# Pooled products with the last 16 keys: four of 32 rows and 72 columns in place of two of 64 padded rows and 144 columns

## The chip, the cores and the metric

The kernel runs on one core of a Trainium2 chip. The metric is the device time of one execution, in microseconds (us), as the median of several. The engines are TensorE (PE; its weight loads are shown apart as PEld), VectorE (DVE), ScalarE (ACT), GpSimd (POOL) and SyncE (SP, which here only issues DMAs).

## What is computed

Attention over 8 batches and 8 heads, 576 positions, 64 elements a head, followed by a layer of two matrix products with a gate. The attention is a sum of two parts: one on sequences pooled by four (144 pooled queries, keys and values), repeated four times, and one inside a band of seven positions.

```python
q_d = q.reshape(B, H, Sd, 4, D).mean(axis=3)      # k_d, v_d alike; Sd = 144
out_d = softmax(q_d @ k_d.T / 8) @ v_d
out_up = np.repeat(out_d, 4, axis=2)
mask = np.abs(pos[:, None] - pos[None, :]) < 4
out_local = softmax(np.where(mask, q @ k.T / 8, -1e9)) @ v
x = (out_up + out_local)                          # to (4608, 512)
h = x @ w_in                                      # 512 -> 2048
out = (h * np.clip(h + 3, 0, 6) / 6) @ w_out      # 2048 -> 512
```

## The kernel before

The attention is done in units: one unit is one batch and a pair of heads, so there are four units in each of the eight batches. The first batch (b = 0) and the second (b = 1) take other paths; from the third batch on (b = 2 to 7, the units for which `alone` is false) 24 units go through the path that the change touches. The two heads of a pair are called h = 0 and 1; their 64 elements lie on the lower and the upper 64 partitions.

A planner (`Plan`) puts all pieces of work in order. Every piece has a cost in us, what it depends on, which buffers it takes and frees, and a due time; the planner simulates five queues with them and then writes out each engine's instructions in that order. The costs are numbers in the calls of `op(...)`.

The expert layers (lines 1065 and 1124) are products of 128 rows and 128 columns on 512 moving columns. Each weight and each activation is split in a high and a low part, so that each product is made of three. Between these, TensorE does the units in bursts (`plan_burst`): one burst does the scores of a new unit and the products with v of a unit that came two before. In the order of the code a burst is:

- `scores_d4` (line 507): the pooled scores of the new unit;
- `pv` (line 747): 20 banded products of the old unit. The window of 57 to 64 keys on one half of the partitions is the row half g of the array, the head h the column half, so that four products in turn use the four quarters;
- `pv_d4` (line 671): the pooled products of the old unit, described below;
- `scores` (line 704): 20 banded scores of the new unit.

The last two bursts have only an old unit, that is `pv` and `pv_d4`.

Between its scores and its products a unit's pooled probabilities are written to DRAM by rows of queries (`put_d`) and fetched back in blocks of 32 by 32 (`get_d`, lines 618 to 631), and DVE turns each block over (`turn_d`, line 633), so that keys lie on partitions. The tile `rd` has 18 blocks of 32 columns. The first 12 hold keys 0 to 127 of both heads, on 128 partitions. Blocks 12 to 17 hold the last 16 keys (`KR`), 16 of head 0 and 16 of head 1 on 32 partitions, with 64 queries in each of three parts, of which 48 (`QB`) are used. The three parts overlap (they begin 40 queries apart, `QSTEP`), and `used` picks the 48.

The pooled values are sums of four rows of v (`ld4` and `sum4`). Part g = 0 has pooled keys 0 to 127. For part g = 1, the last 16 keys, `ld4` (lines 436 to 438) loads the same 16 rows twice, onto partitions 0 to 15 and 16 to 31; `sum4` sums them, multiplies each head's 64 columns by a column of `head` (line 455), which is one on that head's 16 partitions and zero on the other's, and clears rows 32 to 63 (line 456).

`pv_d4` (lines 661 to 673) then does three steps, each for both heads: g = 0 takes keys 0 to 63, g = 1 keys 64 to 127, both with 64 rows and 144 queries, into the two PSUM banks `pod[0]` and `pod[1]`; g = 2 takes the last keys on partitions 0 to 63, rows 32 to 63 being zero, with 144 queries, and adds into `pod[0]`. Heads use the two column halves. The banks are added afterwards by `mean` and `mean_too` (lines 684 to 689).

In the second batch (`mixed`) `pv_d4` does g = 2 with 48 rows instead; the change leaves that as it is.

Of the kernel before, what the change touches and what calls it, by code (L numbers as in the profile page):

```python
# [8 lines left out]
F32 = mybir.dt.float32  # L9
# [5 lines left out]
ALU = mybir.AluOpType  # L15
AX = mybir.AxisListType

B, H, S, D = 8, 8, 576, 64
DM, DFF = 512, 2048
P = 128  # L20
# [7 lines left out]
SD = S // 4  # L28
# [3 lines left out]
ROW = 2 * D  # L32
# [3 lines left out]
NAR = 32  # L36
QS, QSTEP, QB = 64, 40, 48
# [2 lines left out]
QPLACE = ((0, 0), (0, 2), (1, 1)), ((0, 1), (1, 0), (1, 2))  # L40
KR = SD - P
KEEP = NAR + KR
MASKED = -8.0e9
FIRST4 = 4 * STEP // 4
FOURS = FIRST4 + 1 + SD // 2
# [14 lines left out]
def tile_local_down_attention_moe(ctx, tc, q_all, k_all, v_all, _qk_loc, _v_loc, w_in, w_out, ident_d, _mask_d, out):  # L60
# [7 lines left out]
    nc = tc.nc  # L68
# [4 lines left out]
    const = pool("const")  # L73
# [9 lines left out]
    ident = const.tile([P, P], F32, name="ident")  # L83
# [3 lines left out]
    op = plan.op  # L87
# [7 lines left out]
    def buf(key, holder, shape):  # L95

        n = 1
        for k in shape[1:]:
            n *= k
        slot = plan.slot[key, holder]  # L100
        if type(slot[0]) is str:
            tag, first = PLACES[slot[0]]
            if tag not in early:
                early[tag] = wts.tile([P, 2048 if PAIRED[0] <= int(tag[1:]) < PAIRED[1] else 1024], F32, name="early", tag=tag)
            return view(early[tag][:, first + slot[1] // 4:], n, shape)
        at = slot[0]
        if at < XB:
            place = key if key == "rawd" else "xb"
            if place not in early:
                early[place] = mem.tile([P, XB // 4], F32, name="first", tag="first")  # L110
            return view(early[place][:, at // 4:], n, shape)
        t, at = (arena, at - XB) if at < ARENA else (rounded, at - ARENA)
        return view(t[:, at // 4:], n, shape)
# [13 lines left out]

    hot = const.tile([P, P], BF16, name="hot")
    mask = const.tile([P, D], F32, name="mask")
    head = const.tile([NAR, 2], F32, name="head")  # L130

    def scratch():
        if "zz" not in early:
# [30 lines left out]

    def make_head():
        for h in range(2):
            nc.vector.tensor_reduce(out=head[:, h:h + 1], in_=ident[:NAR, h * KR:(h + 1) * KR], op=ALU.add, axis=AX.X)


    win, wout = {}, {}  # L170
# [71 lines left out]
    def src(t, first, ap):  # L242
        return bass.AP(tensor=t.tensor, offset=t.offset + first * ROW, ap=ap)
# [124 lines left out]
    def plan_unit(b, d, u, row0, k0, kv, PS, pair, masked, early_user, due):  # L368
        hp = 2 * d + u
        row0 = row0 + u * S  # L370
        un = b, hp
        st, qk = {}, {}
        s_ops, sd_ops, turned, pooled = [], [], {}, {}

        alone = un < ALONE

        direct = b == 0
        mixed = alone and not direct
# [29 lines left out]
        for kind, t in (("q", q_all), ("k", k_all)):  # L408
            hk = kind, un
            if direct:  # L410
                a = turned[kind] = pair["turned"][kind]
            else:
                l = op("SP", 2.0, partial(ldt, t, kind), loads if b == 1 else [], take=[("qk", hk)], size=dma(4 * S, 128), nd=4, each=0.57)
                a = turned[kind] = [op("DVE", 0.72, partial(turn, kind), [l])]
# [14 lines left out]
        def ld4(g):  # L429
            st["raw", g] = raw = buf("raw" + k0, ("v", un, g), [P, 4, ROW])  # L430
            if g == 0:
                nc.sync.dma_start(raw, src(v_all, row0, [[4 * ROW, P], [1, 4 * ROW]]))
            elif alone:
                nc.sync.dma_start(raw[NAR:KEEP], src(v_all, row0 + 4 * P, [[4 * ROW, KR], [1, 4 * ROW]]))
            else:
                for h in range(2):
                    nc.sync.dma_start(
                        raw[h * KR:(h + 1) * KR], src(v_all, row0 + 4 * P, [[4 * ROW, KR], [1, 4 * ROW]]))

        def sum4(g, eng):  # L440
            if "vd" not in st:
                st["vd"] = buf("vd" + k0, un, [P, 2, ROW])
            ps = slice(NAR, KEEP) if g and alone else slice(0, 2 * KR if g else P)
            raw, vd = raw_of(g)[ps], st["vd"][ps, g]
            if g and alone:
                eng.memset(st["vd"][:NAR, 1], 0.0)
            if eng is nc.vector:
                eng.tensor_reduce(out=vd, in_=raw.rearrange("p r e -> p e r"), op=ALU.add, axis=AX.X)  # L448
            else:
                eng.tensor_tensor(raw[:, 0:2], raw[:, 0:2], raw[:, 2:4], op=ALU.add)  # L450
                eng.tensor_tensor(vd, raw[:, 0], raw[:, 1], op=ALU.add)
            if g and not alone:

                for h in range(2):
                    eng.tensor_scalar(vd[:, h * D:(h + 1) * D], vd[:, h * D:(h + 1) * D], head[:, h:h + 1], None, op0=ALU.mult)
                eng.memset(st["vd"][NAR:D, 1], 0.0)

        def v_of():
            return pair["v"][:, u] if b == 0 else st["v"]
# [156 lines left out]
                    st["pd"][h * D:(h + 1) * D])  # L616

        def get_d():
            st["rd"] = raw = buf("qk", ("rd", un), [P, 18, NAR])
            st["pdt"] = raw.rearrange("p j k -> p (j k)")  # L620
            dd = st["dd"]
            for e in range(4):
                nc.sync.dma_start(
                    raw[e * NAR:(e + 1) * NAR, :12],
                    bass.AP(tensor=dd.tensor, offset=dd.offset + e * NAR, ap=[[SD, NAR], [NAR * SD, 12], [1, NAR]]))
            for h in range(2):
                for i in range(2):
                    nc.sync.dma_start(
                        raw[:NAR, 12 + i::2, h * KR:(h + 1) * KR],
                        bass.AP(tensor=dd.tensor, offset=dd.offset + (h * D + i * NAR) * SD + P,  # L630
                                ap=[[SD, NAR], [2 * D * SD, 3], [1, KR]]))

        def turn_d(i):
            n, a, e = (P, 0, 12 * NAR) if i == 0 else (NAR, 12 * NAR, 18 * NAR)
            x = st["pdt"][:n, a:e]
            nc.vector.transpose(out=x, in_=x)

# [19 lines left out]
        def used(x, first, step):  # L657

            return bass.AP(tensor=x.tensor, offset=x.offset + first, ap=[x.ap[0], [step + QB - QSTEP, 3], [1, QB]])

        def pv_d4():

            st["od"] = buf("od" + k0, un, [P, SD])
            st["pod"] = [st["px"][g][:, HALF:HALF + SD] for g in range(2)]
            for g in (0, 1, 2):
                ks = slice(0, KEEP) if mixed and g == 2 else slice(g % 2 * D, (g % 2 + 1) * D)
                for h in range(2):
                    hs = slice(h * D, (h + 1) * D)
                    w = used(st["pdt"][ks, g // 2], h * D, 2 * D) if mixed else \
                        used(st["pdt"][ks], h * D, 2 * D) if g < 2 else used(st["pdt"][ks], 6 * D, D)  # L670
                    nc.tensor.matmul(  # L671
                        st["pod"][g % 2][hs].rearrange("p (j q) -> p j q", j=3), st["vd"][ks, g // 2, hs],
                        w, start=(g < 2), stop=(g > 0), skip_group_check=True)

        def pv_d():
            st["pod"] = bank(PS, ("od", un))[:, :SD]
# [142 lines left out]
        elif alone:  # L819
            a = op("DVE", 0.52, lambda: top(rows_d(), st["md"]), [sd])  # L820
            sums_d = [op("ACT", 1.6, lambda: weigh(rows_d(), st["pd"], st["md"], st["sd"]), [a], free=[bk])]
        else:
            pulls = [op(on("ev", SD // 2), 0, partial(pull, h, i), [sd], take=[pk], free=[hx[h]]) for h in range(2) for i in range(2)]
            sums_d = []
            for n in (2, 0, 1):
                a = op("DVE", 0.22, lambda n=n: top(rows_d4(n), st["md"][:, n:n + 1]), pulls if n == 2 else [sd])
                sums_d.append(op("ACT", 0.84, partial(weigh4, n), [a], take=[pk], free=[bks[n]] if n != 2 else []))
        a = op("DVE", 0.15, lambda: recip(st["sd"]), sums_d)
        a = op(on("normd" if alone else "norm", 3 * SD), 0, lambda eng: norm(eng, st["pd"], st["sd"]), [a], free=[sk], lock=True)
# [1443 lines left out]
```

## Time and profile before

| | |
|---|---|
| time, median of 3 runs | 879.05 us (878.76 to 880.36) |
| profiled execution | span 877.4 us from the first to the last instruction; no other time is given for it |
| PE busy | 870.0 us (99%), 6964 products |
| PE weight loads | 716.1 us (82%) |
| DVE, ACT, POOL busy | 74%, 56%, 30% |
| chain that ended last | 98% PE |
| DMA | 136.40 MB, 155 GB/s over the span |

Times in the profile are from the start of the span. An f32 product shows as two records (each with its weight load), a product of the split kind as one. Records of products overlap, since products are pipelined: the distance between starts, or the pieces of the chain, tell how fast they follow each other, not the duration of a record. A form such as `64*64 64x144` is: 64 rows by 64 columns of the array, 64 partitions by 144 moving columns.

### The profile page before, as it was taken

To read this page: it belongs to the slowest core of one execution; us is meant where nothing else is said; L and a number is where in the kernel's file an instruction comes from. 1 tells how busy PE (TensorE), PEld (TensorE's weight loads), DVE (VectorE), ACT (ScalarE), POOL (GpSimd) and SP (SyncE) were. 2 spreads that over 40 slices of the span, in tenths; PEclk is the share of its full clock that TensorE was granted. 3 is DMA by queue.
4 is the path that set the end of the run, shared out by engine and by line. 5 is a ranking of instruction groups with operands and counts; after the bars stand their busy time and mean duration, and the time that the engine had idled before them with its cause. 6 is when DMAs were issued, how large, how long until landed. Compare 5 with 4: busy or idle time off the path is not lost.

```text
span 877.4 us, 19829 instructions
## 1 busy us (share of the span) xinstructions
PE 870.0 (99%) x6964; PEld 716.1 (82%) x6964; DVE 651.5 (74%) x1235; ACT 494.3 (56%) x1557; POOL 264.3 (30%) x396
## 2 busy tenths in 40 slices
PE   8999999999999999999999999999999999999998
PEld 5788888888888888888888888888888888888887
DVE  7997976766876787667766776667856768778984
ACT  5998856575564555545454555555552325556760
POOL 6646542423324331344323431433422110000000
PEclk9999999999999999999999999999999999999999
DMA  9899253675766665656465647677864116674794
GB/s 250 238 312 254 65 129 89 126 142 117 147 155 132 138 125 129 130 118 135 100 156 127 134 105 167 133 195 221 195 148 104 37 39 234 207 227 145 268 274 71
DMA packets 358735, 136.40 MB, mean 155 GB/s; under 512 B 269612, under 2 KB 331180, under 8 KB 358636
## 3 DMA queue, kind: packets, MB, share of 16 engines
q1 hardware_dynamic: 353052, 134.22, 61.7%
q10 hardware_dynamic: 5584, 0.92, 0.6%
q8 instruction: 55, 0.90, 0.4%
q14 instruction: 44, 0.36, 0.1%
HBM read 90.44 MB, written 44.63 MB: 154 GB/s over the span
## 4 chain that ended last, share of the span: by engine, by line
PE 98%; DMA 0%; DVE 0%; issue 0%; SPq 0%; ACT 0%
PE o L1124 36%; PE h L1065 35%; PE a L1381 4%; PE h L1381 4%; PE o L1644 4%; PE o L1491 2%; PE a L704 2%; PE h L747 2%; PE a L507 1%; PE h L1644 1%; PE a L1644 1%; PE h L671 1%; DMA arena<-in_q_dram 0%; PE a L597 0%; PE h L507 0%; PE a L747 0%
## 5 line engine op out<-in xcount | busy, mean ns | idle before, releaser
L1124 PE MATMUL o<-wp,rounded 128*128 128x512 f32 x1344 | 323.6, 392 | 0.0
L1065 PE MATMUL h<-rounded,wp 128*128 128x512 f32 x1344 | 315.9, 390 | 0.0
L1065 PEld LDWEIGHTS h<-rounded,wp 128*128 128x128 f32 x1344 | 251.5, 188 | 52.6 <-issue 0.4
L1124 PEld LDWEIGHTS o<-wp,rounded 128*128 128x128 f32 x1344 | 249.6, 188 | 53.7 <-issue 1.0
L1075 DVE SCALAR_TENSOR_TENSOR arena<-arena,h 128x512 f32<-128x512 f32 x112 | 75.8, 677 | 54.9 <-ACT arena L1071 54.0
L1071 ACT ACTIVATE arena<-h 128x512 f32<-128x512 f32 x112 | 66.6, 595 | 83.3 <-PE h L1065 76.0
L1079 ACT CAST rounded<-arena 128x512 fp32r<-128x512 f32 x112 | 68.9, 616 | 63.3 <-PE o L1124 39.5
L1083 DVE TENSOR_TENSOR rounded<-arena,rounded 128x512 fp32r<-128x512 f32 x78 | 57.3, 735 | 48.5 <-PE o L1124 41.7
L571 ACT ACTIVATE arena<-arena 128x64 f32<-128x64 f32 x240 | 80.1, 336 | 0.4
L1083 POOL TENSOR_TENSOR rounded<-arena,rounded 128x512 fp32r<-128x512 f32 x34 | 46.2, 1359 | 96.8 <-PE o L1124 48.7
L1187 POOL TENSOR_TENSOR arena<-arena 128x128 f32<-128x128 f32 x65 | 33.1, 510 | 67.5 <-DVE arena L1187 38.6
L391 DVE STREAM_TRANSPOSE arena<-arena 128x576 f32<-128x576 f32 x56 | 42.8, 767 | 4.4 <-DMA arena<-in_q_dram 2.7
L571 ACT ACTIVATION_READ_ACCUMULATOR arena<-arena 128x1 f32 x240 | 45.3, 189 | 0.0
L547 ACT ACTIVATE arena<-arena 128x1 f32<-128x1 f32 (+1 forms) x77 | 14.9, 194 | 52.8 <-DVE arena L560 52.6
L450 POOL TENSOR_TENSOR arena<-arena 32x256 f32<-32x256 f32 (+2 forms) x28 | 21.4, 763 | 74.7 <-DMA arena<-in_v_dram 74.5
L685 ACT ACTIVATE arena<-h 128x144 f32<-128x144 f32 x24 | 7.0, 291 | 64.7 <-PE h L671 64.7
L448 DVE TENSOR_REDUCE arena<-arena 128x128 f32<-128x512 f32 (+2 forms) x28 | 29.7, 1063 | 6.9 <-PE h L671 5.6
L581 DVE RECIPROCAL arena<-arena 128x10 f32<-128x10 f32 (+1 forms) x60 | 11.4, 190 | 29.0 <-ACT arena L557 16.5
L588 DVE TENSOR_TENSOR arena<-arena 128x640 f32<-128x640 f32 (+1 forms) x38 | 31.8, 836 | 1.1
L560 DVE TENSOR_REDUCE arena<-arena 128x10 f32<-128x640 f32 (+1 forms) x57 | 31.3, 553 | 0.2
L406 POOL TENSOR_TENSOR arena<-arena 128x144 f32<-128x144 f32 x52 | 29.9, 575 | 4.1
L1381 PE MATMUL h<-wp,wp 128*128 128x512 f32 x120 | 30.0, 389 | 0.0
(286 smaller groups left out, 1371.0 us busy)
## 6 DMA issues: line engine op xcount, KB each, us to landing
rawp<-in_w_in_dram SPq DMA_DIRECT2D x16, 512.0 KB
rawp<-in_w_out_dram SPq DMA_DIRECT2D x16, 512.0 KB
arena<-in_q_dram SPq DMA_DIRECT2D x112, 72.0 KB
arena<-in_k_dram SPq DMA_DIRECT2D x112, 72.0 KB
pl<-arena SPq DMA_DIRECT2D x24, 320.0 KB
arena<-pl SPq DMA_DIRECT2D x96, 80.0 KB
arena<-in_v_dram SPq DMA_DIRECT2D x28, 256.0 KB
wd<-wp SPq DMA_DIRECT2D x12, 512.0 KB
```

The costliest lines, as they stand in the source:

```text
L391: nc.vector.transpose(out=qk[kind], in_=qk[kind])
L571: nc.scalar.activation(x[:, j], x[:, j], AF.Exp, bias=m[:, j:j + 1], scale=0.125, accum_out=s[:, j:j + 1])
L588: eng.tensor_tensor(x, x, s.unsqueeze(2).broadcast_to(list(x.shape)), op=ALU.mult)
L1065: nc.tensor.matmul(st["ps"], win[f][:, wt, kk * P:(kk + 1) * P], xs[part][:, kk], start=(kk == 0 and i == 0), stop=(kk == NK - 1 and i == ...
L1071: nc.scalar.activation(st["t"], st["ps"], AF.Relu, bias=3.0)
L1075: nc.vector.scalar_tensor_tensor(out=t, in0=t, scalar=6.0, in1=st["ps"], op0=ALU.min, op1=ALU.mult)
L1079: nc.scalar.copy(st["gh"], st["t"])
L1083: eng.tensor_tensor(st["gl"], st["t"], st["gh"].bitcast(F32), op=ALU.subtract)
L1124: nc.tensor.matmul(otile[n, m], gt[:, ms], wout[f][:, wt], start=(f == 0 and i == 0), stop=(f == NF - 1 and i == 2),)
L1187: eng.tensor_tensor(u[:, z], u[:, x], u[:, y], op=o)
L1381: nc.tensor.matmul(ps, weight(i, j, wt, kk), xpart(MOVING[j], part)[:, kk], start=first and kk == 0 and x == 0, stop=kk == half - 1 and x ...
L1644: nc.tensor.matmul(places[acc, m][:, ts], w, z[:, part, ts], start=j == 5 and i == 0 and x == 0, stop=i == NG - 1 and x == 2, skip_group_c ...
```

## The change

The last 16 keys are laid out twice: the first half of the queries of each part (24, `QH`) with its keys on partitions 0 to 31, the second half on partitions 64 to 95. The values of the last 16 keys are loaded to both places. `pv_d4` then does g = 2 with 32 rows from partition 0 and 72 queries (the first 24 of each part) into `pod[0]`, and g = 3 with 32 rows from partition 64 and the other 72 queries into `pod[1]`, each for both heads. Rows 32 to 63 are read by no product any more and are not cleared. `turn_d` turns 96 partitions by 96 columns in place of 32 by 192, `rd` has 15 blocks, and `sum4` works on 96 partitions for g = 1. All costs and dependences given to the planner stay as they are.

```diff
+QH = QB // 2
...
-    head = const.tile([NAR, 2], F32, name="head")
+    head = const.tile([P, 2], F32, name="head")
...
-            nc.vector.tensor_reduce(out=head[:, h:h + 1], in_=ident[:NAR, h * KR:(h + 1) * KR], op=ALU.add, axis=AX.X)
+            nc.vector.tensor_reduce(
+                out=head[:, h:h + 1], in_=ident.rearrange("p (g k) -> p g k", g=2)[:, :, h * KR:(h + 1) * KR], op=ALU.add, axis=AX.XY)
...
-                for h in range(2):
+                for i in range(2):
                     nc.sync.dma_start(
-                        raw[h * KR:(h + 1) * KR], src(v_all, row0 + 4 * P, [[4 * ROW, KR], [1, 4 * ROW]]))
+                        raw[i * D:i * D + NAR], src(v_all, row0 + 4 * P, [[0, 2], [4 * ROW, KR], [1, 4 * ROW]]))
...
-            ps = slice(NAR, KEEP) if g and alone else slice(0, 2 * KR if g else P)
+            ps = slice(NAR, KEEP) if g and alone else slice(0, D + NAR if g else P)
...
-                    eng.tensor_scalar(vd[:, h * D:(h + 1) * D], vd[:, h * D:(h + 1) * D], head[:, h:h + 1], None, op0=ALU.mult)
-                eng.memset(st["vd"][NAR:D, 1], 0.0)
+                    eng.tensor_scalar(vd[:, h * D:(h + 1) * D], vd[:, h * D:(h + 1) * D], head[ps, h:h + 1], None, op0=ALU.mult)
...
-            st["rd"] = raw = buf("qk", ("rd", un), [P, 18, NAR])
+            st["rd"] = raw = buf("qk", ("rd", un), [P, 15, NAR])
...
-                        raw[:NAR, 12 + i::2, h * KR:(h + 1) * KR],
-                        bass.AP(tensor=dd.tensor, offset=dd.offset + (h * D + i * NAR) * SD + P,
-                                ap=[[SD, NAR], [2 * D * SD, 3], [1, KR]]))
+                        raw[i * D:i * D + QH, 12:, h * KR:(h + 1) * KR],
+                        bass.AP(tensor=dd.tensor, offset=dd.offset + (h * D + i * QH) * SD + P,
+                                ap=[[SD, QH], [(2 * D + QB - QSTEP) * SD, 3], [1, KR]]))
...
-            n, a, e = (P, 0, 12 * NAR) if i == 0 else (NAR, 12 * NAR, 18 * NAR)
+            n, a, e = (P, 0, 12 * NAR) if i == 0 else (D + NAR, 12 * NAR, 15 * NAR)
...
-            for g in (0, 1, 2):
-                ks = slice(0, KEEP) if mixed and g == 2 else slice(g % 2 * D, (g % 2 + 1) * D)
+            for g in (0, 1, 2) if mixed else range(4):
+                n = KEEP if g == 2 and mixed else D if g < 2 else NAR
+                ks = slice(g % 2 * D, g % 2 * D + n)
                 for h in range(2):
                     hs = slice(h * D, (h + 1) * D)
-                    w = used(st["pdt"][ks, g // 2], h * D, 2 * D) if mixed else \
-                        used(st["pdt"][ks], h * D, 2 * D) if g < 2 else used(st["pdt"][ks], 6 * D, D)
+                    to = st["pod"][g % 2][hs].rearrange("p (j q) -> p j q", j=3)
+                    if g < 2 or mixed:
+                        w = used(st["pdt"][ks, g // 2] if mixed else st["pdt"][ks], h * D, 2 * D)
+                    else:
+                        w = st["rd"][ks, 12:, :QH]
+                        to = to[:, :, g % 2 * QH:(g % 2 + 1) * QH]
                     nc.tensor.matmul(
-                        st["pod"][g % 2][hs].rearrange("p (j q) -> p j q", j=3), st["vd"][ks, g // 2, hs],
-                        w, start=(g < 2), stop=(g > 0), skip_group_check=True)
+                        to, st["vd"][ks, g // 2, hs], w, start=(g < 2), stop=(g == 1 if mixed else g > 1) or g == 2, skip_group_check=True)
```

## Rows read from the trace of the kernel before

**Rows 1.** The page: busy time with share and instructions, granted clock, DMA totals.

```profile
PE 870.0 (99%) x6964; PEld 716.1 (82%) x6964; DVE 651.5 (74%) x1235; ACT 494.3 (56%) x1557; POOL 264.3 (30%) x396
...
PEclk9999999999999999999999999999999999999999
...
DMA packets 358735, 136.40 MB, mean 155 GB/s; under 512 B 269612, under 2 KB 331180, under 8 KB 358636
```

**Rows 2.** Stretches, PE alone: length, busy time and count, clock, DMA.

```profile
160.00:691.00 531.00, 531.00 (x4578) 1.00 0.62 139
691.00:873.70 182.70, 182.70 (x828) 1.00 0.57 176
```

**Rows 3.** Chain of waits around a burst: start, us, line and count.

```profile
301.17 2.72 PE o L1124 x12
...
306.07 2.95 PE o L1124 x12
...
330.83 0.41 PE a L507 x8
331.24 0.13 PE h L507 x8
331.36 0.58 PE h L747 x40
331.94 0.36 PE h L671 x10
332.30 0.04 PE a L704
332.34 0.09 PE h L671 x2
332.43 0.58 PE a L704 x29
```

**Rows 4.** Chain of waits, the last burst, which has no scores.

```profile
689.69 0.74 PE h L747 x40
690.43 0.48 PE h L671 x12
```

**Rows 5.** Chain of waits, a burst with scores alone.

```profile
138.02 0.58 PE a L704 x40
```

**Rows 6.** Lines 704 and 671, 160 to 691 us: durations, starts, forms.

```profile
L704 PE MATMUL a<-arena x880: 216/218/268, 168.6 to 647.0; 64*64 64x64 f32 x176
...
L671 PE MATMUL h<-arena x288: 282/283/294, 168.3 to 690.6; 64*64 64x144 f32 x144
```

**Rows 7.** Chain of waits, pooled products of the first and second batch.

```profile
34.52 0.64 PE a L682 x8
...
61.59 0.48 PE a L671 x12
```

**Rows 8.** Order of time on PE: start, us from first start to last end.

```profile
28.40 0.29 PE L682 MATMUL o<-early 72*64 72x144 f32 x1
28.61 0.27 PE L747 MATMUL o<-early 64*64 64x60 f32 x2
...
61.66 0.41 PE L671 MATMUL a<-first,arena 48*64 48x144 f32 x4
```

**Rows 9.** Groups by line and form: busy us, mean ns, idle time before.

```profile
L636 DVE STREAM_TRANSPOSE arena<-arena 128x384 f32<-128x384 f32 x24 | 13.7, 570 | 0.0
...
L450 POOL TENSOR_TENSOR arena<-arena 32x256 f32<-32x256 f32 x20 | 15.1, 756 | 73.0 <-DMA arena<-in_v_dram 73.0
...
L636 DVE STREAM_TRANSPOSE arena<-arena 32x192 f32<-32x192 f32 x24 | 7.8, 326 | 0.4 <-DMA arena<-pd 0.4
...
L450 POOL TENSOR_TENSOR arena<-arena 128x256 f32<-128x256 f32 x5 | 4.1, 812 | 1.5 <-DMA arena<-in_v_dram 1.5
```

**Rows 10.** Who waited for line 437's loads: us in all, times.

```profile
  POOL arena L450: 73.0, 8
```

**Rows 11.** DMA issues: line, count, KB each.

```profile
arena<-in_v_dram SPq DMA_DIRECT2D x80, 32.0 KB
```

## The prediction

> **What bounds the kernel now.** I read the page first: TensorE (PE) is busy for 870.0 of 877.4 us, no other engine for more than 74%, and PEclk stands at 9 in every slice, so all of what follows is at full clock [rows 1]. Busy time of PE is modelled, so I next asked for stretches: from 160 to 691 us, where all 24 changed units fall, PE is busy for 531.00 of 531.00 us, and from there to 873.7 for 182.70 of 182.70 [rows 2]. Then the chain of waits: from the first changed burst on it names nothing but PE lines, back to back; the reader sees in it one burst between two pieces of the expert layers, and no wait for DVE, ACT, POOL or a DMA [rows 3]. The kernel is therefore bound by the length of PE's own instruction stream. A change to that stream counts in full and everything else has slack. What matters is how long PE needs for the pooled products of a burst.
>
> In the chain a piece runs from the end of the piece before it to its own end, which makes lengths comparable. A burst runs: pooled scores (L507), banded products (L747), pooled products (L671), banded scores (L704). Each f32 product shows as two records. Four products in four different quarters of the array run side by side: 40 records of L747 take 0.58 us, or ten rounds of 0.058 [rows 3].
>
> **Pooled products without any other effect.** Before: first 128 keys, four products in four quarters; then the last 16 keys, two products, both in the upper row half, 144 columns. Twelve records take 0.48 us where nothing interleaves [rows 4], which is four rounds of 0.12, two for the first four products and two for the last two. After: the last keys are four products of 72 columns, one in each quarter. The price of that form is shown by L507 h, four products of 64x72 in the four quarters: 8 records in 0.13 us, against 0.24 for 144 columns [rows 3]. So I count 0.24 - 0.12 = 0.12 us less per burst. Does L704, which slips four records into the idle lower half, give this back? With the interleaving L704 takes 0.04 + 0.58 = 0.62 [rows 3]; a burst without pooled products takes 0.58 for all 40 records [rows 5]. The early start buys nothing, so the saving stays at 0.12 in both places. 24 bursts hold L671 (288 records at 12 each), 22 of them with L704 behind (880 records at 40 each) [rows 6].
>
> **What the change adds on PE: another tile height.** All products around it use 64 rows by 64 columns. The new ones use 32 rows. Nothing in this trace uses 32-row products, so the cost of going there and back must be bounded.
>
> Upper side: each time the kernel changes the shape in which the array is cut, PE loses time with no semaphore behind it. (a) From 128x128 products to 64x64 ones: L747 takes 0.74 us where it starts a burst [rows 4] and 0.58 inside one [rows 3], so 0.16 us. (b) The same step into L507: 0.41 for two rounds worth 0.24 [rows 3], 0.17. (c) From 64x64 (L747) to 72*64 products, whose 72 rows need the taller cut at equal columns: L682 takes 0.64 us for 8 records, two side by side, so four rounds worth 0.48, again 0.16 [rows 7]. (d) Back from 72*64 to 64x64: starts 0.21 us apart (28.40 to 28.61), where a round takes 0.12, so 0.09 of emptying before any exposed weight load [rows 8]. (e) From 64x64 to 128x128: L1124 x12 takes 2.95 behind a burst and 2.72 elsewhere, 0.23 [rows 3], with weights twice as wide.
>
> Lower side: a smaller row count alone costs nothing. In the bursts of batch 2 the last-key products have 48 rows [rows 8], and the twelve records take 0.48 us as where all have 64 [rows 7]. If 32 rows are to the array what 48 are, the switch is 0; nothing there suggests a gain beyond the 0.12.
>
> I take 0.16 per switch, by (a) to (c): 48 rows still fit a 64-row cut and 72 don't fit it; that is where the rows show the loss, and (c) is the nearest row, a change of height alone at 64 columns. 32 rows, cut in strips of their own, are such a change. The range keeps 0 and 0.23.
>
> Trainium skill, "TensorEngine Tiling (Array Packing)", section "Key Properties": going from one tiling mode to another (not from tile to tile) empties the engine; its "Available Configurations" list 32x64 apart from 64x64. The trace agrees for every change of cut that it holds (0.09 to 0.23 us, rows 3, 4, 7, 8); none of them is 64 to 32. By it the sum is the one below.
>
> **Sum.** In each of the 22 bursts with L704 behind there are two added switches: 2 x 0.16 - 0.12 = +0.20 us. In the last two bursts the array goes to 128x128 behind the pooled products anyway, so one switch is added: 0.16 - 0.12 = +0.04. 22 x 0.20 + 2 x 0.04 = 4.5 us. Profiled span 877.4 + 4.5 = 881.9. The page gives the profiled execution as its span only; the median of the runs, 879.05, stands 1.65 above it (what lies around the span), which doesn't change. Forecast: 883.5 us, 0.5% slower.
>
> **The other edits, all beside PE.**
> - Turning the last keys (L636): 32x192 becomes 96x96 on DVE. 32x192 takes 326 ns and 128x384 570 [rows 9]: with 192 columns more, 244 ns or 1.27 a column, so 96 columns take about 204 ns, an estimate from these two rows; 0.12 us less, 24 times. DVE isn't on the chain [rows 3]: 0 on the time.
> - Sums of v (L448 to L456): 96 partitions instead of 32 at equal width, and one memset less. POOL takes 756 ns for 32x256 and 812 for 128x256 [rows 9], so up to 56 more in L450; by the same ratio, 1.07, the other POOL operations of the unit grow by less than that each, and DVE's by the two rows above not at all. Bounds per unit: 0 (the memset pays for it) and 0.2 us, for four operations at 56 ns. The cover is POOL's idle time, 70% of the span by the page; without it 24 x 0.2 = 4.8 us. Value: 0.
> - Loads of v (L437): two issues of 32 KB [rows 11] become two of 64 KB, 1.5 MB more over 24 units. At the mean 155 GB/s [rows 1] 64 KB more take 0.4 us longer to land. POOL stands in L450 for these loads for 73.0 us in all, in 8 waits [rows 10], and what is queued behind on POOL (L451, L455, some L1083) stands with it; L1083's result is what PE needs next. Without cover that is 24 x 0.4 = 9.9 us. But those 8 waits of about 9 us each leave no mark on PE [rows 2], so 0.4 more stays hidden: 0.
> - Fetching probabilities (L628): still four issues, with 72 short runs each for 96. The SP queue issues as many as before and moves fewer bytes: 0.
> - head (L167) is made once, at the start, and gets wider by a hundred elements: 0. The cost terms that set the order are untouched, so nothing is moved past another queue.
> - Two more products per burst are 4 matmul records more, 96 on 6964 [rows 1], each with its weight load. PE never stood for its instructions between 160 and 873 us [rows 2]: 0.
>
> **Rivals.**
> 1. *The switch is free* (32 rows behave in a 64-row cut as 48 do). For it: the 48 rows [rows 7, 8], and the gapless moves between quarters [rows 3]. Against it: every crossing of a tile height in the trace costs [rows 4, 7, 8]. Time: 24 x -0.12 = -2.9, 876.2 us, faster. It decides as soon as a switch costs under 0.06 us. Trainium skill, "TensorE: Matmul & The Clock Gate", section "Part 3: Packing small matmuls — row/col tiling": slices that start at partition multiples of 32 land in row groups of their own and run together, with no word of a price for coming from another size. That the quarters run together the trace agrees (0.058 us a round, rows 3); the price is what it leaves open, and by this rule alone the sum would be this rival's. Chance 0.14.
> 2. *Only the emptying is paid*, 0.09 (d), and the weights are loaded meanwhile: 2 x 0.09 - 0.12 = +0.06, and -0.03 in the last two: 22 x 0.06 - 0.06 = 1.3 us, 880.3. For it: the load of the next weights runs beside products elsewhere. Against it: (a) to (c), 0.16 each. Chance 0.09.
> 3. *The four small products don't run side by side*, eight rounds of 0.06 instead of two: 0.37 more in each of 24 bursts, 4.5 + 8.9 = 13.4, 892.5. Against it: products on different quarters do so everywhere here. Chance 0.03.
>
> The forecast has 0.74.
>
> **How the numbers follow.** The measurement can tell about 0.2% (1.8 us) from no change. Slower by more: the forecast and rival 3, 0.77 (the forecast's own spread stays above). Within: rival 2, 0.09. Faster: rival 1, 0.14. The range leaves out rivals 1 and 3 (0.17), begins at rival 2, 880.2, and ends at 885.0, where a switch costs 0.19 in place of 0.16; 0.23 each, the end (e), would be 886.6, but its weights are twice as wide.
>
> **What the trace after would show.** L671 with twelve records at 64 rows as eight, and eight new ones at 32 rows and 72 columns; between the last 64-row and the first 32-row record 0.21 us (0.12 + 0.09), and 0.15 from there to the first L704. The pieces of the chain from L507 to the last L704 sum to 2.19 us before [rows 3], 2.39 after. No L1124 or L1065 piece outside a burst longer than before, no wait for POOL or DVE on the chain. If they sum to 2.07, rival 1 is right; at 2.25, rival 2. The forecast is also wrong if PE stands for POOL behind L450.

## The result, and the profile after

The changed kernel takes 887.74 us (median of 6 runs, 885.33 to 889.67), beside 879.56 us for the kernel before on the same chip: 0.9% slower, ratio 1.0091, 95% interval 1.0077 to 1.0105. The forecast was 883.5 us, its range ended at 885.0. The direction was right, the size was not: some 4 us more were lost than the sum had, and they don't lie in PE's own products, as the traces show.

In the changed kernel the lines are 1 to 6 higher: pooled scores L508, banded products L752, pooled products L677, banded scores L709, expert layers L1070 and L1129, loads of v L439, their sums on DVE L450 and on POOL L452, the addition that empties a PSUM buffer L757.

The page of the profiled execution (887.77 us, span 885.9), its line of busy times, as in [rows 1]:

```profile
PE 876.8 (99%) x7060; PEld 716.6 (81%) x7060; DVE 646.9 (73%) x1231; ACT 494.0 (56%) x1557; POOL 263.0 (30%) x376
```

PE is busy for 6.8 us more than before, the span is 8.5 us longer: part of the loss is idle time of PE, which [rows 2] did not have. Not all of the 6.8 us is more work: at the start of this execution the granted clock stood at 0.50 for 3.4 us (length, busy and count, granted clock, DMA share, GB/s):

```profile
16.80:20.20 3.40, 3.37 (x28) 0.50 1.04 343
```

In the trace before, the same stretch is at 1.00. By half the 3.37 us, an estimate, this is 1.7 us of busy time. The chain of waits around the burst that stands in [rows 3] (start, us, line, count):

```profile
333.28 0.41 PE a L508 x8
333.69 0.12 PE h L508 x8
333.81 0.58 PE h L752 x40
334.39 0.54 PE h L677 x16
334.93 0.74 PE a L709 x40
```

The pieces sum to 2.39 us, the forecast's number; 2.19 before. The rise stands where it was put: L677 takes 0.54 though it holds less work, and L709 0.74 for what took 0.62 [rows 3]; the 0.12 more is the way back to 64 rows, 0.16, less the 0.04 of the interleaving. The two distances that the prediction named can be read from the starts of the records: the last one of 64 rows starts at 334.36 us and the first one of 32 rows at 334.57, which is 0.21; from the last one of 32 rows (334.71) to the first of L709 (334.86) it is 0.15. The first four of 32 rows in order of time (start, us, line, form):

```profile
334.57 0.29 PE L677 MATMUL h<-arena 32*64 32x72 f32 x4
```

Matched product by product against the trace before, each of the 22 bursts moves what follows by 0.205 to 0.208 us more. The last burst, without scores:

```profile
697.70 0.74 PE h L752 x40
698.43 0.54 PE h L677 x16
```

From 697.70 to the next product at 698.97 this is 1.27 us, for 1.22 [rows 4]: +0.05, where the forecast had 0.04. So PE's stream grew by 4.6 us, as predicted (4.5).

The rest appears in the stretches for PE alone, which have holes where [rows 2] had none:

```profile
160.00:674.00 514.00, 514.00 (x4479) 1.00 0.64 142
674.00:682.00 8.00, 6.20 (x76) 1.00 0.78 189
682.00:693.00 11.00, 11.00 (x50) 1.00 0.17 49
```

1.8 us of PE are empty between 674 and 682. The waits of PE (what waited, for whom, us in all, times, longest):

```profile
PE h L1070 <- DVE arena L757: 1.0, 1, 1.0
PE h L752 <- DVE arena L1080: 0.8, 1, 0.8
```

And the chain in that stretch, which leaves PE there (between 160 and 663 us it names PE lines alone, as the chain before does from 160 to 691):

```profile
663.44 4.63 DMA arena<-si
...
669.52 3.11 DMA arena<-si
...
674.18 3.19 DMA so<-arena
...
678.01 0.41 DVE arena L1187
...
679.27 0.97 DVE arena L450
...
680.49 0.47 DVE arena L757
...
681.09 5.72 PE h L1070 x24
```

Read it backwards: PE (L1070) stands for an addition on DVE (L757), which is queued behind a sum of v (L450) and a sum of expert weights (L1187), which waits for a transfer, and that for one whose first part SP issued at 663.44. The issue just ahead of it on SP is the last changed load of v. In the trace before SP came to this transfer at 653.06, 10.4 us earlier, while PE was only 5.4 us earlier there; so SP's queue had fallen back by some 5 us more than PE.

The 8.4 us between the two traces, by the start offsets of the products with 512 moving columns: 0.9 before 41 us (the stretch with the lower clock lies there; the other runs' traces stand between -0.9 and +1.2 at that point, so it is taken as scatter of the start), 4.5 in 22 bursts, 0.1 in the last two, 1.1 and 1.3 in the two waits (with PE's restart), 0.2 at 658 us, 0.4 behind the last burst (rounded pieces).

### The profile page after: what moved, and what is told of

Same layout as the page of the kernel before. It is cut to its first block, busy times and chain, and to the rows that moved or that the text cites. A ratio compares the mean times of both kernels' runs of the same rounds, so it can differ in the third digit from the quotient of the medians.

```text
span 885.9 us, 20022 instructions
## 1 busy us (share of the span) xinstructions
PE 876.8 (99%) x7060; PEld 716.6 (81%) x7060; DVE 646.9 (73%) x1231; ACT 494.0 (56%) x1557; POOL 263.0 (30%) x376
## 4 chain that ended last, share of the span: by engine, by line
PE 96%; DMA 2%; DVE 1%; issue 0%; ACT 0%; SPq 0%; ACTq 0%
PE o L1129 34%; PE h L1070 34%; PE a L1386 4%; PE h L1386 4%; PE o L1649 4%; PE o L1496 2%; PE a L709 2%; PE h L752 2%; PE h L677 1%; PE a L508 1%; PE h L1649 1%; PE a L1649 1%; DMA arena<-si 1%; DMA arena<-in_k_dram 1%; PE a L598 0%
## 5 line engine op out<-in xcount | busy, mean ns | idle before, releaser
L1129 PE MATMUL o<-wp,rounded 128*128 128x512 f32 x1344 | 323.6, 393 | 0.0
L1070 PE MATMUL h<-rounded,wp 128*128 128x512 f32 x1344 | 316.3, 391 | 1.0 <-DVE arena L757 1.0
L1070 PEld LDWEIGHTS h<-rounded,wp 128*128 128x128 f32 x1344 | 251.5, 188 | 54.3 <-issue 2.1
L1129 PEld LDWEIGHTS o<-wp,rounded 128*128 128x128 f32 x1344 | 249.9, 188 | 53.1 <-issue 0.6
L452 POOL TENSOR_TENSOR arena<-arena 96x256 f32<-96x256 f32 (+2 forms) x28 | 21.6, 771 | 112.4 <-DMA arena<-in_v_dram 76.0
L450 DVE TENSOR_REDUCE arena<-arena 128x128 f32<-128x512 f32 (+2 forms) x28 | 29.9, 1068 | 9.4 <-PE h L677 5.6
```

The costliest lines, as they stand in the source:

```text
L1070: nc.tensor.matmul(st["ps"], win[f][:, wt, kk * P:(kk + 1) * P], xs[part][:, kk], start=(kk == 0 and i == 0), stop=(kk == NK - 1 and i == ...
L1129: nc.tensor.matmul(otile[n, m], gt[:, ms], wout[f][:, wt], start=(f == 0 and i == 0), stop=(f == NF - 1 and i == 2),)
```

## The experiments

Each was timed in five rounds beside the kernel before; "us" is the median of 5 to 12 runs. "Cost" is the ratio less one, times 879.05 us.

| run | what | us | ratio, 95% interval | cost, us |
|---|---|---|---|---|
| after | the change | 887.74 | 1.0091 [1.0077, 1.0105] | +8.0 |
| e1_rows32 | before, last keys on 32 rows | 886.21 | 1.0077 [1.0065, 1.0089] | +6.8 |
| e2_pad64 | after, all products 64 rows | 883.56 | 1.0051 [1.0039, 1.0064] | +4.5 |
| e3_delay | before, longer burst, no switch | 884.93 | 1.0062 [1.0050, 1.0074] | +5.5 |
| e4_side | the edits beside PE alone | 883.60 | 1.0043 [1.0029, 1.0057] | +3.8 |
| e5_loads | only the new loads of v | 885.30 | 1.0073 [1.0053, 1.0093] | +6.4 |
| e6_noloads | e4 with the old loads | 879.23 | 0.9998 [0.9987, 1.0008] | -0.2 |
| e7_plain | 64 KB loads of distinct rows | 879.68 | 1.0005 [0.9996, 1.0013] | +0.4 |
| e8_copy | e2 with old loads, copy on chip | 876.78 | 0.9979 [0.9969, 0.9988] | -1.8 |
| e9_four | before, four plain 32 KB loads | 882.93 | 1.0043 [1.0027, 1.0059] | +3.8 |
| e10_after4 | after, four plain loads | 883.97 | 1.0053 [1.0040, 1.0065] | +4.7 |
| e11_pad4 | e2 with four plain loads | 877.99 | 0.9979 [0.9970, 0.9987] | -1.8 |
| e12_order | e5, step of zero inside | 879.93 | 1.0001 [0.9991, 1.0011] | +0.1 |

**Is the price of the tile height real?** The kernel before, its two last-key products on 32 rows instead of 64, nothing else (144 columns, the padding is simply left out):

```
-                ks = slice(0, KEEP) if mixed and g == 2 else slice(g % 2 * D, (g % 2 + 1) * D)
+                ks = slice(0, KEEP) if mixed and g == 2 else slice(0, NAR) if g == 2 else slice(g * D, (g + 1) * D)
```

> The kernel before, but the two products with the last 16 keys use 32 rows in place of 64 (the padding rows were zero, so the result is the same); 144 columns, loads, turns and sums as before. Theory A (each step between 64-row and 32-row products costs PE about 0.15 to 0.16 us; the waits seen at 655 to 681 us in the changed kernel come from its edits beside PE): a burst is 0.33 us longer (0.21 as in the changed kernel plus the 0.12 that its narrower products saved), 22 x 0.33 + 2 x 0.17 = 7.5 us, 887.0, and no wait on PE around 670. Theory B (those waits come from PE being late against the transfers): 7.5 plus 2 to 3.5, 889 to 891, with waits around 670. Theory C (32 rows cost nothing; the columns or the number of products do): 879.5.

886.21 us, and between 160 and 873 us its trace has no wait of PE, as before. The chain around the same burst:

```profile
333.67 0.64 PE h L671 x12
334.32 0.74 PE a L704 x40
```

Each burst moves what follows by 0.313 us, each of the last two by 0.16: two switches and one, 0.16 each, with equal work. 22 x 0.313 + 2 x 0.16 = 7.2; the timing gives 6.8. Rival 1 (the switch is free) falls here, and so does rival 2 (0.09 each).

**What is left without it.** The changed kernel with 64 rows in all products, the padding set to zero:

```
-                n = KEEP if g == 2 and mixed else D if g < 2 else NAR
+                n = KEEP if g == 2 and mixed else D
```

> The changed kernel, but its four products with the last 16 keys use 64 rows, the added ones cleared to zero, so no product has 32 rows; all edits beside PE stay (two small memsets and 32 more partitions of a turn are added). Theory A: a burst is 0.12 us shorter than before, 24 x 0.12 = 2.9 us, and the edits beside PE add their waits of 2 to 3.5 us: 878.5 to 880. If the edits beside PE are harmless (theory B): 876.6 and no waits around 670. Theory C: as slow as the changed kernel, 887.7.

A miss: each burst is 0.113 us shorter than before, as the forecast's 0.12 has it, and yet the time is 883.56. (That the burst shrinks also shows that four small products run side by side, against rival 3.) In its trace PE loses 2.1 us to waits between 306 and 333 and 1.2 us at 673, both behind DVE (a gate of the experts, and the addition that empties a PSUM buffer). The profiled execution took 880.10 us, 3.5 less than the median, so the others lost more than these waits show. The side edits cost something by themselves; whether they cost more because the bursts are shorter is not shown.

**Does a later PE cause the waits?** The kernel before with its first four banded products of a burst done twice: PE's stream grows without switches or side edits.

```
-            for jj in range(5):
+            for jj in range(5) if alone else (0, 1, 0, 1, 2, 3, 4):
```

> The kernel before, with the first eight of the 20 banded products of a burst done twice (same result), so PE is later by about as much as in the changed kernel, without 32 rows and without the edits beside PE. Four rounds of 0.058 us in 24 bursts are 5.6 us. Theory A: 885.1, no wait on PE around 670. Theory B: 887 to 889, with waits there.

884.93 us: 0.233 per burst, the banded products' piece 0.81 instead of 0.58, and no wait of PE between 160 and 873 us. Lateness alone brings none.

**The edits beside PE alone.** All of the change except the products, which stay two of 64 rows and 144 columns and read other probabilities, so the pooled part of the output is not the reference's:

```
-                n = KEEP if g == 2 and mixed else D if g < 2 else NAR
+                n = KEEP if g == 2 and mixed else D
...
-                        w = st["rd"][ks, 12:, :QH]
+                        w = used(st["pdt"][ks], 7 * QB, QSTEP)
```

> The changed kernel with its edits beside PE (double loads, 96 partitions of sums and turns) but PE's products as before: two of 64 rows and 144 columns; they read other columns, so the pooled part of the output is not the reference's. Theory A: the bursts are 2.497 us as before and waits of 2 to 3.5 us appear on PE: 881.5 to 883. Theory B: 879.5, no waits on PE.

883.60 us, with bursts as before and PE waits at 634, 650, 670 and 673 us. The chain to the first of them:

```profile
626.99 0.69 SPq L439
...
627.72 5.39 DMA arena<-in_v_dram
...
633.14 1.03 DVE arena L450
...
634.61 0.61 DVE arena L1079
...
635.26 5.74 PE h L1069 x24
```

The sum on DVE, in order of time, with the idle time before it in brackets:

```profile
633.14 1.02 DVE L450 TENSOR_REDUCE arena<-arena 96x128 f32<-96x512 f32 x1 [2.83 <-DMA arena<-in_v_dram]
```

Now it is plain: a changed load of v is issued (0.69 us), takes 5.39 us to land, the sum on DVE (L450) waits for it, the gate of the expert layer (L1079, queued behind on DVE) reads PE's result late, and PE stands for it. 3.8 here and 4.6 on PE make 8.4; the change measures 8.0.

**Loads or the rest?** The kernel before with only the new loads, and the fourth experiment with the old ones:

```
-                for h in range(2):
-                    nc.sync.dma_start(
-                        raw[h * KR:(h + 1) * KR], src(v_all, row0 + 4 * P, [[4 * ROW, KR], [1, 4 * ROW]]))
+                for i in range(2):
+                    nc.sync.dma_start(
+                        raw[i * D:i * D + NAR], src(v_all, row0 + 4 * P, [[0, 2], [4 * ROW, KR], [1, 4 * ROW]]))
```

> The kernel before with one edit of the change alone: the two loads of the last 16 rows of v put 32 rows each (64 KB, through the added step of zero that reads the rows twice), the second to partitions 64 to 95, where nothing reads it. Theory L (the 4.1 us of the edits beside PE come from these loads): 883.5, with PE standing for DVE. Theory R (they come from the fetches, turns and sums): 879.5.

> All edits beside PE as in e4_side (products as before, pooled part of the output not the reference's), but the loads of v as before, 32 KB each, so that the rows summed on partitions 64 to 95 are old data. Theory L: 879.5, no wait of PE. Theory R: 883.5.

885.30 with the loads alone, 879.23 with everything but them: these two instructions per unit are the whole loss beside PE. They cost more alone (6.4) than inside e4 (3.8), though the two intervals overlap. Waits of PE in the fifth's trace (this execution took 889.37 us, 4 more than the median):

```profile
PE h L1065 <- DVE arena L752: 2.3, 1, 2.3
PE h L747 <- DVE arena L1075: 2.3, 1, 2.3
PE h L1065 <- DVE arena L1075: 1.1, 2, 0.6
```

The first of them in order of time on DVE (start, us, line, operation), first the kernel before, then the fifth experiment:

```profile
284.06 1.03 DVE L448 TENSOR_REDUCE arena<-arena 128x128 f32<-128x512 f32 x1
...
286.07 0.81 DVE L752 TENSOR_TENSOR arena<-h,arena 128x288 f32<-128x288 f32 x2
```

```profile
286.53 0.78 DVE L391 STREAM_TRANSPOSE arena<-arena 128x576 f32<-128x576 f32 x1 [0.65 <-DMA arena<-in_k_dram]
287.31 1.02 DVE L448 TENSOR_REDUCE arena<-arena 128x128 f32<-128x512 f32 x1
...
289.12 0.81 DVE L752 TENSOR_TENSOR arena<-h,arena 128x288 f32<-128x288 f32 x2
```

Before, the first of the two additions L752 ends at 286.52 and PE has other products until 287.57: about 0.9 us to spare, with the 0.14 that PE takes to start. That is all the cover there is at this place. With the new loads DVE is 3.05 us later, and PE waits 2.3. DVE itself stands there for a load of k (L391), which SP issues late: SP begins the four loads of k at 280.81 us, before at 277.10. The chain goes back over several links of SP, DVE and ACT to a changed load of v:

```profile
266.57 5.10 DMA arena<-in_v_dram
```

The wait costs more than its length: stretches for PE around it (granted clock is the column behind the count):

```profile
280.00:289.50 9.50, 7.44 (x131) 1.00 0.78 188
289.50:292.50 3.00, 2.79 (x7) 0.51 0.80 132
292.50:300.00 7.50, 7.50 (x34) 0.97 0.45 88
```

After 2.3 us without work the clock stands at 0.51, the lower of its two levels (1.2 GHz), and the first seven products go at half speed: 2.79 us, where twelve take 2.72 [rows 3], so about 1.2 us are lost on top of the wait. The same comes once more, behind the second wait of 2.3 us:

```profile
678.60:682.10 3.50, 3.50 (x19) 0.51 0.34 78
```

In this execution the lower clock is part of what it loses beyond e4_side, whose trace stands at 1.00 from 160 to 870 us.

**The bytes, or the form of the load?** The same 64 KB to the same places in the same number of loads, but 32 different rows of v in each (other rows of v for the last keys, so the pooled part is not the reference's):

```
-                        raw[i * D:i * D + NAR], src(v_all, row0 + 4 * P, [[0, 2], [4 * ROW, KR], [1, 4 * ROW]]))
+                        raw[i * D:i * D + NAR], src(v_all, row0 + 4 * (SD - NAR), [[4 * ROW, NAR], [1, 4 * ROW]]))
```

> As e5_loads, the same 64 KB to the same places, but as 32 different rows read once, without the step of zero (the wrong rows of v for the last keys, so the output differs). If theory L holds through the bytes and where they land: 883.5 as e5_loads. If it holds through the time that SP needs to issue a load (0.69 us in place of 0.43, should the step of zero be what makes it longer): issue back near 0.45 and 880 to 881.

879.68 us, with one new wait of PE, 0.4 us. The bytes cost nothing that the timing can tell; the form does. What differs is seen in the DMA's share over time (tenths in 40 slices of 0.19 us, and GB/s). The stretch around one pair of loads, in the fifth experiment, from 422.5 to 430 us:

```profile
DMA  8899999988589944019999611111111111100000
GB/s 129 135 176 288 322 311 298 232 175 169 191 328 382 371 153 22 0 44 279 309 328 298 186 66 44 44 66 44 44 66 44 38 44 44 44 27 0 0 0 0
```

When everything else has landed, the two loads drag on for 12 slices, 2.3 us, at 38 to 66 GB/s (44 in most) and at a tenth of the 16 engines. In the seventh experiment and in the kernel before the same place has no such tail; the kernel before, from 418.5 to 426 us:

```profile
DMA  9999999888899848999710000000000000000000
```

And the packets of the fifth, beside [rows 1]:

```profile
DMA packets 358831, 137.97 MB, mean 155 GB/s; under 512 B 268940, under 2 KB 330508, under 8 KB 358732
```

672 fewer under 512 bytes than before, 14 for each of the 48 loads, though nothing small was taken out. A load that marks its end once on each of 16 engines and now on two would lose just 14. That reading of the count is an inference; the share of a tenth (2 of 16 is 0.125) agrees with it, and so does e9_four below, which has 48 plain loads more than the kernel before and 270380 small packets, 768 or 16 a load more.

**Copy instead of loading twice.** The second experiment with the old loads; the second 32 rows are copied on the chip:

```
+            if g and not alone:
+                eng.memset(st["vd"][:, 1], 0.0)
...
+                copy_on(eng, st["vd"][D:D + NAR, 1], vd)
```

> Four products of 64 rows (as e2_pad64) with the loads of v as before; the summed rows are copied from partitions 0 to 31 to 64 to 95 by the engine that summed them, and the buffer is cleared first. Theory L: bursts of 2.383 us, 24 x -0.113 = -2.7, 876.8, no wait of PE. If the copy (0.2 to 0.45 us on DVE or POOL for each unit) makes those late: 878 to 880. Theory R: 880 to 881.

876.78 us: 0.2% faster than the kernel before, and faster than the changed one. From 60 us on its trace has no wait of PE. The pooled products and the scores in its chain:

```profile
331.82 0.38 PE h L680 x16
332.20 0.58 PE a L712 x40
```

**Four plain loads of 32 KB**, first in the kernel before, then in the changed kernel, then in the second experiment:

```
-                    nc.sync.dma_start(
-                        raw[i * D:i * D + NAR], src(v_all, row0 + 4 * P, [[0, 2], [4 * ROW, KR], [1, 4 * ROW]]))
+                    for h in range(2):
+                        nc.sync.dma_start(
+                            raw[i * D + h * KR:i * D + (h + 1) * KR], src(v_all, row0 + 4 * P, [[4 * ROW, KR], [1, 4 * ROW]]))
```

> The kernel before with the two loads of the last 16 rows of v replaced by four plain ones of 16 rows (32 KB each), to the same four places that the change fills: as many bytes as e5_loads, no step of zero. Theory T (the loads with the step of zero are slow to land, because they leave most DMA engines unused): 879.3 to 880, as before. Theory I (SP's issue time is what makes them late): four issues of 0.43 us are 1.72 us a unit, against 1.38 in e5_loads and 0.86 before, so at least as slow as e5_loads, 885 or more.

> The changed kernel, its products of 32 rows kept, with four plain loads of 16 rows in place of the two with the step of zero. Theory T: only the steps between 64 and 32 rows are left, 22 x 0.207 + 2 x 0.052 = 4.6 us over before, 883.9, PE waiting for nothing. Theory I: 887 to 891.

> Four products of 64 rows (e2_pad64) with four plain loads. Theory T: 22 x -0.113 - 2 x 0.11 = -2.7 us, 876.6, about as e8_copy. Theory I: 882 or more.

The changed kernel with plain loads takes 883.97 us: the forecast's sum, to half a microsecond. The padded one takes 877.99, 5.6 less than with the loads that the change has. In the kernel before, four loads cost 3.8 us, which neither theory had (nothing, or 6 and more); those runs lie between 880.11 and 886.22, and the profiled one, the fastest, has no new wait of PE, so where that time goes is not shown. The padded kernel's trace shows what it can be: PE waits 1.9 us behind DVE at the place at 287 us that e5_loads showed, because DVE stands for a load of v:

```profile
285.80 1.03 DVE L451 TENSOR_REDUCE arena<-arena 128x128 f32<-128x512 f32 x1 [1.41 <-DMA arena<-in_v_dram]
```

and the chain behind that load is SP, issuing back to back from 267.67 us. Two more issues per unit are 0.8 us more on that queue.

**The order of the steps.** The fifth experiment with the step of zero as the second dimension: two copies inside, 16 keys outside (the copies come to lie row by row, so the last keys' part mixes the heads' rows):

```
-                        raw[i * D:i * D + NAR], src(v_all, row0 + 4 * P, [[0, 2], [4 * ROW, KR], [1, 4 * ROW]]))
+                        raw[i * D:i * D + NAR], src(v_all, row0 + 4 * P, [[4 * ROW, KR], [0, 2], [1, 4 * ROW]]))
```

> The kernel before with the changed loads of v, as in the fifth experiment (885.30), but with the step of zero in the second place of the list of steps: 16 keys first, two copies inside. Same 64 KB, same number of loads, same zero step, same rows of SBUF; the copies come to lie row by row next to each other instead of half by half, so the last keys' part of the pooled output mixes the heads' rows. Theory L (the outer dimension decides over how many of the 16 DMA engines a load is spread: two when it is two long): the load is spread over 16 again, the count of packets under 512 bytes is 269612 as before, the tail of some 3 us at 44 GB/s is gone, the issue takes about 0.43 us, and the time is 879.3 to 880 us. Theory Z (reading the same rows twice makes the load slow, in whatever order): 884 to 887 us, with the tail. If the packets spread but the issue stays at 0.69 us: 880 to 882 us, by the experiment with four plain loads, whose issues together took 0.9 us more per unit and cost 3.4 us.

879.93 us, ratio 1.0001: theory L. The tail is gone and the small packets are back at the 269612 of [rows 1]. The expected issue of 0.43 us did not come: an issue takes 612 ns in the middle, nearer to the 687 of the fifth experiment than to the 428 before, and since the time is as before, this much issue time is covered. The issues (ns least, middle, most), then the DMA's share from 418.5 to 426 us:

```profile
L437 SPq DMA_DIRECT2D arena<-in_v_dram x48: 585/612/841, 112.8 to 653.9; - x48
```

```profile
DMA  7999999899989718899993000000000000000000
```

The slow thing is an outer dimension of length two, not reading twice, not the bytes.

The Trainium skill, "DMA: Bandwidth & Descriptors", section "Why a DMA increments its semaphore by 16 and not by 1", states it: the number of engines that a transfer uses is the largest up to 16 that divides the length of the slowest dimension on both sides; its section "Rules for kernel authors" names a leading broadcast of zero step as the case that confines a transfer. By that rule the changed loads run on two engines, and the plain ones of 16 and 32 rows on 16. The traces agree: 14 small packets less per load, a tenth of the engines busy. The prediction had cited other pages and not this one.

## Why the prediction was wrong, point by point

- *What bounds the kernel*: right. PE's stream was the bound, and e3_delay shows that a longer stream counts in full (0.233 for a piece longer by 0.23, nothing else).
- *0.12 less for four small products*: right, 0.113 in each burst of e2_pad64 and e8_copy.
- *0.16 per change of the tile height*: right. e1_rows32 has 0.313 for two and 0.16 for one; after against e2_pad64 0.32 for two. The marks named in advance came: 0.21 us into the 32-row products and 0.15 out of them, 2.39 for the chain of the burst. The doubt whether 32 rows behave like 48 is settled: 48 rows cost nothing [rows 8], 32 do.
- *Turning the last keys, wider sums, fetching, head at nothing*: right, e6_noloads, 0.9998. *Two more products at nothing* wasn't tried apart; e8_copy holds them and is faster.
- *Loads of v: "64 KB more take 0.4 us longer to land ... so 0.4 more stays hidden: 0"*: **this step failed**, and it is the whole miss. Three errors stand in it. The size: 0.4 us is 64 KB at the mean rate of all traffic [rows 1]; a pair of these loads drags 2.3 us behind the rest, and each issue takes 0.69 us instead of 0.43. I counted bytes and never looked at the shape of the load, which the diff shows plainly (`[0, 2]` in front). The queue: I looked for those who wait on POOL [rows 10]; PE came to stand behind DVE, which has the gates and the additions that empty PSUM in one queue with sums of v and with other work that waits for what SP issues behind these loads. The cover: "those 8 waits leave no mark on PE" [rows 2] says that the slack isn't negative, not how large it is. It was 0.9 us at the place of the first long wait in e5_loads.

Who waited for these loads in the changed kernel (us in all, times), where [rows 10] had POOL alone behind a sum of v:

```profile
  POOL arena L452: 76.0, 13
  DVE arena L450: 2.9, 3
```

The bound without cover, 9.9 us, was named and then kept out of the range, because the forecast gave the cover full trust. The right sum would have been 4.6 on PE plus 3.3 to 3.8 for the loads (after against e10_after4, and e4_side), 7.9 to 8.4; measured 8.0. One slip in the sums changes nothing: 0.23 for each switch would give 886.8 us, not 886.6.

The changed shape of the products isn't lost for that: with all products at 64 rows and the second copy made on the chip (e8_copy) it takes 876.78 us, 0.2% less than before (0.9979, 0.9969 to 0.9988) and by the medians 1.2% less than the change as made.

Open: why four plain loads cost 3.8 us in the kernel before and next to nothing in the changed one. Longer bursts, which give DVE and SP more time, don't explain it: the bursts of e11_pad4 are shorter than before, and it has the same ratio as e8_copy, which has no such loads. Open too: how the loss in the changed kernel divides between landing and SP's queue at 663 us; what is left, beside the clock, of the difference between e4_side and e5_loads.

## What to carry to other kernels

Where one engine is busy all the time, "no wait in the profile" is a slack of unknown size: before an edit beside it is costed at nothing, find the place where its result is needed soonest, in every queue that it passes, and read how many tenths of a microsecond are left. Judge a transfer by its outermost dimension and its issue, not by its bytes: here loads of the same 64 KB cost 6.4 us in all with two copies outside and 0.1 with them inside. A smaller tile among larger ones pays twice, going and coming back, 0.16 us each; padded to the size of its neighbours it keeps what its columns save and pays neither.

## What was not expected of the hardware

- A pair of loads whose outer dimension is two long fell to 44 GB/s, where the traffic before it moved 300 (e5_loads).
- After 2.3 us without work PE went on at a granted clock of 0.51 for the next seven products, in the fifth experiment at 289.5 us; [rows 2] had 1.00. The length of the wait alone doesn't tell it: at the start of the changed kernel's trace the clock stood at 0.50 behind a wait of 1.5 us (16.8 us), and in the kernel before it kept 1.00 there behind one of 2.0 us.
- 32 rows in an array cut for 64 cost 0.16 us each way, with the same columns; the 48 rows of [rows 8] cost nothing.
